# Attention and two feed-forward layers on one core: value matmuls one item later, rotation work moved, fewer weight tiles converted during attention

## The chip, the cores and the metric

One core of one Trainium2 chip runs the whole program in one launch. The metric is device time in microseconds (us). Engines are named as in the profile: PE (TensorE, with PEld for its weight loads), DVE (VectorE), ACT (ScalarE), POOL (GpSimd), SP (SyncE, which here issues all DMAs).

## What is computed

Attention over 4 batches x 8 heads x 576 positions x 64, with rotary positions, then two feed-forward layers on 2304 tokens of 512, hidden size 2048. All in fp32.

```python
def _attn_ref(q, k, v):                       # rotate(x): halves x1, x2 -> x1*cos - x2*sin, x1*sin + x2*cos
    q_rot, k_rot = (rotate(q), rotate(k))
    scores = scale * np.matmul(q_rot, k_rot.transpose(0, 1, 3, 2))
    scores = scores - np.max(scores, axis=-1, keepdims=True)
    attn = np.exp(scores)
    attn = attn / (np.sum(attn, axis=-1, keepdims=True) + 1e-09)
    return np.matmul(attn, v)
x = attention as (2304, 512)
h = x @ w_in;   g = where(h > 0, h, exp(min(h, 0)) - 1);   x = g @ w_out      # first layer
h = x @ w2_in;  g = h - tanh(h);                           out = g @ w2_out   # second layer
```

## The kernel before

The program has two stages, and in both the order of every instruction is written out by hand; each engine takes its own instructions in that order.

**Attention.** The 32 heads go in 16 pairs (`p`). A pair has 9 items (`items`, L207 and below): 128 query rows of one head each, for four row blocks `u` and two heads, and a last item with the 64 rows that remain of both heads. In the loop over items, iteration `i` does for different items, in this order: the maximum of item `i` on DVE (`emit_max`, L220), the score matmuls of item `i + 1` on PE (`emit_s`, L211; ten matmuls in a pair's last item, four in the others), the exponential of item `i` on ACT (`emit_exp`, L234), the copies of transposed scores out of PSUM that the iteration before left (`flush`, on DVE at L265 or ACT at L267), the sums' reciprocals on DVE and the normalizing on POOL for item `i - 1` (`emit_norm`, L247 to L251, only after a pair of heads is complete), rotation and conversion steps, the transposes of item `i - 4` on PE (`emit_t`, L291, the corners at L304 and L297), and value matmuls that are due (`emit_pv`, L325). There are two PSUM tiles for scores, three for transposes and one for the values' output. `PV_AT` says how many iterations after the transposes of a group of items its value matmuls stand: for each of five pieces of 128 keys a number.

```python
            PV_AT = ((1, 1, 1, 3, 3), (1, 1, 1, 3, 3), (2, 2, 2, 2, 2))
```

The rotation of q and k (`prep`) has five steps for each pair and each of q (`x` = 0) and k (`x` = 1): two multiplications with the tables on POOL (L146), an addition on DVE (L148), a rounded copy on ACT (L151), the rest on DVE (L156), and then DMAs that put the result into its operand tiles (`place`, L178 and L181). `sched` says in which iteration each stands, `early` does so for the first two pairs after the start.

**Weights.** The weights come as 64-bit numbers, in 64 tiles of 128 x 512. `load_w` loads a raw tile; `conv_w` makes fp32 of it and splits it into two fp32r parts, in `NCV` = 5 parts: absolute value on ACT (L83), two operations on DVE (L85, L86), one (L90), one (L94), and last a rounding on ACT (L102) with the remainder on POOL (L103). The eight tiles that the first layer needs first are converted during attention, one for every two pairs of heads, one part in every second iteration.

**Feed-forward.** A step is one block of 128 hidden units for 384 tokens: `emit_f1` (L445, 12 matmuls), the activation on ACT and DVE, the split of its result `g` on ACT and POOL (`emit_split`), and four steps later `emit_f2` (L503). Four steps share a token tile. The tokens' operands `x1` to `x5` are made from the attention's output during the first steps (`split_x`, ACT at L54 and POOL at L55): step `i` makes piece `i % 4` of token tile `i // 4 + 1`. Meanwhile the other 56 tiles are converted, a tile in three steps.

## Time and profile before

| | |
|---|---|
| median of 3 runs | 1132.71 us (1131.9 to 1133.64) |
| profiled execution | 1132.65 us, span 1130.9 us |
| PE busy | 1097.3 us (97%) |
| DVE, ACT, POOL busy | 765.6, 688.6, 671.3 us |
| chain that ended last, by engine | PE 90%, DVE 5%, DMA 2%, ACT 2% |
| attention stage | the first 318.6 us of the span |

The profile is of one execution. Times in the trace are in us from the span's start. "Busy" for PE includes matmuls whose operands are late, since matmuls are pipelined and their ends are modelled; how fast PE really goes is read from how often a given instruction comes round. A wait is named by what ended it.

### The profile page before, as it was taken

Reading aid. Unit: us, or ns where it says so; the run is one execution under the profiler, and the core shown is the slowest. Engines: PE = TensorE matmul, PEld = TensorE weight load, DVE = VectorE, ACT = ScalarE, POOL = GpSimd, SP = SyncE. Lnnn points to the kernel's source line nnn. Section 1 sums busy time; section 2 is a strip of 40 time slices with the busy share of each in tenths; the row PEclk is TensorE's granted clock in tenths of the full one; section 3 lists DMA queues with packets and bytes.
Section 4 is the critical chain, followed back from the end, with each engine's and each line's share of the span. In section 5 each row is a group of like instructions: output and inputs, shape, how many; then the busy total and the mean of one; then the engine's idle time right before and its main releaser. Section 6 shows DMA issues by size and latency. Waiting matters only on the chain.

```text
span 1130.9 us, 18518 instructions
## 1 busy us (share of the span) xinstructions
PE 1097.3 (97%) x6656; PEld 987.2 (87%) x6656; DVE 765.6 (68%) x1393; ACT 688.6 (61%) x1477; POOL 671.3 (59%) x609
## 2 busy tenths in 40 slices
PE   2899999999999999999999999999999999999998
PEld 2777776777799999999999999998998899899987
DVE  6988888888645434555545556678768877877665
ACT  3676766676745533333333344688888788877774
POOL 2877887887556533333333466676666666666443
PEclk9999999999999999999999999999999999999999
DMA  7767676865211111112111121111111111110102
GB/s 232 217 193 200 181 215 169 222 172 164 72 39 38 40 55 38 38 38 55 40 38 38 38 57 38 39 38 38 57 38 38 38 56 38 38 39 1 57 35 78
DMA packets 29627, 91.96 MB, mean 81 GB/s; under 512 B 4192, under 2 KB 4192, under 8 KB 29536
## 3 DMA queue, kind: packets, MB, share of 16 engines
q1 hardware_dynamic: 29536, 90.78, 28.3%
q8 instruction: 53, 0.87, 0.3%
q14 instruction: 38, 0.31, 0.1%
HBM read 57.74 MB, written 4.72 MB: 55 GB/s over the span
## 4 chain that ended last, share of the span: by engine, by line
PE 90%; DVE 5%; DMA 2%; ACT 2%; SPq 1%; issue 1%; ACTq 0%; DVEq 0%
PE h L445 36%; PE y L503 18%; PE y L505 17%; PE o L325 8%; PE s L211 6%; PE pt L291 4%; DVE nm L220 2%; DMA k<-hl 1%; ACT a L234 1%; DVE t L148 1%; DVE aT L265 1%; ACT aT L267 1%; DVE hl L156 0%; DMA tabs<-in_tab 0%; PE pr L304 0%
## 5 line engine op out<-in xcount | busy, mean ns | idle before, releaser
L445 PE MATMUL h<-x,w 128*128 128x384 f32 x2304 | 434.0, 336 | 0.0
L445 PEld LDWEIGHTS h<-x,w 128*128 128x128 f32 x2304 | 407.1, 188 | 8.0 <-ACT a L234 0.4
L488 POOL TENSOR_TENSOR g<-f,g 128x384 fp32r<-128x384 f32 x192 | 213.6, 1113 | 187.8 <-ACT g L487 182.5
L503 PE MATMUL y<-g,w 128*128 128x384 f32 x1152 | 219.0, 339 | 0.0
L505 PE MATMUL y<-w,g 128*128 128x512 f32 x864 | 216.7, 395 | 0.2 <-ACT xa L520 0.2
L503 PEld LDWEIGHTS y<-g,w 128*128 128x128 f32 x1152 | 204.0, 188 | 0.0
L505 PEld LDWEIGHTS y<-w,g 128*128 128x128 f32 x864 | 161.5, 188 | 31.9 <-ACT xa L520 0.6
L251 POOL TENSOR_SCALAR a<-a,r 128x576 f32<-128x576 f32 x144 | 135.2, 951 | 63.7 <-DVE r L248 43.6
L464 POOL TENSOR_TENSOR w<-w,u 128x384 f32<-128x384 f32 x96 | 105.4, 1098 | 99.7 <-ACT w L463 99.7
L234 ACT ACTIVATE a<-s,nm 128x576 f32<-128x576 f32 x144 | 107.1, 743 | 89.6 <-DVE nm L220 75.1
L487 ACT CAST g<-f 128x384 fp32r<-128x384 f32 x192 | 98.0, 510 | 94.1 <-PE y L503 92.4
L475 DVE TENSOR_SCALAR f<-f 128x384 f32<-128x384 f32 x96 | 40.0, 416 | 145.4 <-ACT f L456 145.4
L456 ACT ACTIVATE f<-h 128x384 f32<-128x384 f32 x96 | 47.2, 492 | 146.7 <-PE h L445 143.8
L220 DVE TENSOR_REDUCE nm<-s 128x1 f32<-128x576 f32 x144 | 108.2, 753 | 38.1 <-PE s L211 36.5
L103 POOL TENSOR_TENSOR w<-f,w 128x512 fp32r<-128x512 f32 x64 | 82.6, 1291 | 54.4 <-ACT w L102 54.3
L522 DVE TENSOR_TENSOR xa<-y,xa 128x384 f32<-128x384 f32 (+1 forms) x126 | 74.0, 612 | 47.3 <-PE y L503 42.0
L479 DVE TENSOR_TENSOR f<-h,f 128x384 f32<-128x384 f32 x96 | 53.1, 553 | 68.3 <-ACT f L465 67.8
L481 DVE COPY_PREDICATED f<-mask,w 128x384 f32<-128x384 uint32 x96 | 92.2, 961 | 10.3 <-DVE w L480 0.5
L325 PE MATMUL o<-aT,v 128*64 128x256 f32 (+1 forms) x768 | 89.3, 339 | 2.6 <-ACT aT L267 2.4
L146 POOL TENSOR_TENSOR t<-t,tabs 128x576 f32<-128x576 f32 x59 | 86.3, 1463 | 8.2 <-DMA t<-in_qk 8.2
L291 PE MATMUL pt<-ident,a 128*128 128x128 f32 x576 | 88.3, 277 | 0.1
L461 ACT ACTIVATE u<-h 128x384 f32<-128x384 f32 x96 | 47.4, 494 | 66.4 <-PE h L445 52.1
(55 smaller groups left out, 1379.2 us busy)
## 6 DMA issues: line engine op xcount, KB each, us to landing
k<-hl SPq DMA_DIRECT2D x64, 288.0 KB, 4.2
t<-in_qk SPq DMA_DIRECT2D x30, 576.0 KB, 6.2
raw<-in_w1i SPq DMA_DIRECT2D x16, 512.0 KB, 3.7
raw<-in_w1o SPq DMA_DIRECT2D x16, 512.0 KB, 3.7
raw<-in_w2i SPq DMA_DIRECT2D x16, 512.0 KB, 3.6
raw<-in_w2o SPq DMA_DIRECT2D x16, 512.0 KB, 3.6
v<-in_v SPq DMA_DIRECT2D x16, 288.0 KB, 4.7
qa<-hl SPq DMA_DIRECT2D x32, 144.0 KB, 4.0
```

The lines of the kernel that those rows point to most:

```text
L220: nc.vector.tensor_reduce(out=nm, in_=s_t[i][:, :, 0:288], axis=AX.XY, op=ALU.max, negate=True)
L234: nc.scalar.activation(out=a.rearrange("p (x c) -> p x c", x=2), in_=s[:, :, 0:288], func=AF.Exp, bias=nm_t.pop(i), scale=1.0, accum_out=den,)
L251: nc.gpsimd.tensor_scalar(out=a, in0=a, scalar1=r[:, x:x + 1], scalar2=1.0, op0=ALU.mult, op1=ALU.mult)
L291: nc.tensor.transpose(pt[:, c, :], a[:, h or 0, c0:c0 + 128], ident)
L325: nc.tensor.matmul(out=o[sl, 0:n], lhsT=w, rhs=m, start=(c == 0), stop=(c == 4))
L445: nc.tensor.matmul(out=hp, lhsT=w[:, wp, ws], rhs=x_t[t][:, xp, c, :], start=(m == 0), stop=(m == 3 * KC - 1))
L464: nc.gpsimd.tensor_tensor(out=w, in0=w, in1=u, op=ALU.mult)
L481: nc.vector.copy_predicated(f, mask.bitcast(U32), w)
L487: nc.scalar.copy(out=g[:, 0, :], in_=f)
L488: nc.gpsimd.tensor_tensor(out=g[:, 1, :], in0=f, in1=g[:, 0, :].bitcast(F32), op=ALU.subtract)
L503: nc.tensor.matmul(out=y_t[e][:, 0:NB], lhsT=w[:, wp, es], rhs=gt[:, gp, :], start=st, stop=sp)
L505: nc.tensor.matmul(out=y_t[e], lhsT=gt[:, gp, es], rhs=w[:, wp, :], start=st, stop=sp)
```

## The change

The diff, cut to its core:

```diff
-    NCV = 5
+    NCV = 6
     def conv_w(key, slot, part):
...
         elif part == 1:
             nc.vector.tensor_scalar(out=f, in0=f, scalar1=LO_CLAMP, scalar2=HI_CLAMP, op0=ALU.max, op1=ALU.min)
+        elif part == 2:
             nc.vector.tensor_scalar(
                 out=fu, in0=fu, scalar1=3, scalar2=0x3FFFFFFF, op0=ALU.logical_shift_left, op1=ALU.bitwise_and
             )
...
+    conv = [(0, kind, c) for kind in range(2) for c in range(NJ)]
+    conv += [(l, kind, NJ * g + j) for l in range(2) for g in range(NG) for j in range(NJ) for kind in range(2)][2 * NJ:]
+    NFIRST = NJ + 1
...
-        first_w = [(0, kind, c) for c in range(NJ) for kind in range(2)]
+
+        CYC, CV_AT = 28, (5, 8, 12, 17, 21, 24)
...
-                when = [i0 + o for o in ((-10, -6, -4, -3, -2, -1), (-7, -2, 0, 2, 3, 4))[x]]
+                when = [i0 + o for o in ((-10, -7, -6, -4, -3, -2), (-7, -2, -1, 1, 2, 3))[x]]
...
-            PV_AT = ((1, 1, 1, 3, 3), (1, 1, 1, 3, 3), (2, 2, 2, 2, 2))
+            PV_AT = ((2, 2, 2, 4, 4), (2, 2, 2, 4, 4), (3, 3, 3, 3, 3))
...
-                if i == 1 or i % (2 * NI) == 12:
-                    load_w(first_w[nw.pop()]) if nw else None
+                key, at = divmod(i, CYC)
+                key = conv[key] if key < NFIRST else None
+                if key and at == 0:
+                    load_w(key)
...
-                    c = NI * (p % 2) + r - 3
-                    if c >= 0 and c % 2 == 0 and c // 2 < NCV and p // 2 < len(first_w):
-                        key = first_w[p // 2]
-                        conv_w(key, key[2], c // 2)
+                    if key and at in CV_AT:
+                        conv_w(key, key[2], CV_AT.index(at))
...
-    conv = [(l, kind, NJ * g + j) for l in range(2) for g in range(NG) for j in range(NJ) for kind in range(2)]
-    conv = conv[2 * NJ:]
+    conv = conv[NFIRST:]
...
-            while nload < len(conv) and nload <= i // 3:
-                load_w(conv[nload])
-                nload += 1
-            while ndone < len(todo) and ndone < (i - 2) * NCV // 3:
+            upto = NCV * min(i + 1, 2 * NJ - NFIRST) + max(0, (i - 2) * NCV // 3)
+            while ndone < min(len(todo), upto):
+                while nload < len(conv) and nload <= ndone // NCV + 1:
+                    load_w(conv[nload])
+                    nload += 1
```

A conversion has six parts now, each with one DVE instruction at most. Five tiles are converted during attention, one in 28 items; the remaining three are converted whole in steps 0, 1 and 2 of the first layer, and the other 56 at the old rate. All value matmuls stand one item later. The rotation's DVE steps stand in iterations 5 and 7 (q) and 1 and 3 (k) of a pair; reciprocals stand in iterations 0, 2, 4, 6 and 8. The line numbers of the changed kernel are some six higher.

In attention, on PE: one pair's rows from its seventh transposes on. `s` are scores, `pt` and `pr` transposes, `o` the values' output; `qa0` and `qb0` are the two heads' queries. Before:

```order
L325 MATMUL o_709<-aT2_699,v_286 64x64 x8
L325 MATMUL o_709<-aTr2_700,v_286 64x64 x2
L211 MATMUL s_783<-k1_482,qb0_98 128x288 x4
L291 MATMUL pt_801<-ident_93,a_665 128x128 x4
L211 MATMUL s_810<-k0_479,qa0_96 128x288 x4
L211 MATMUL s_810<-k1_482,qb0_98 128x288 x2
L211 MATMUL s_810<-k1_482,qb0_98 128x224 x2
```

And in the changed kernel:

```order
L217 MATMUL s_761<-k1_469,qb0_98 128x288 x4
L297 MATMUL pt_782<-ident_93,a_656 128x128 x4
L331 MATMUL o_735<-aT_595,v_284 64x256 x2
L331 MATMUL o_735<-aTr_596,v_284 64x256 x2
L331 MATMUL o_735<-aT2_700,v_284 64x64 x8
L331 MATMUL o_735<-aTr2_701,v_284 64x64 x2
L217 MATMUL s_805<-k0_466,qa0_96 128x288 x4
L217 MATMUL s_805<-k1_469,qb0_98 128x288 x2
L217 MATMUL s_805<-k1_469,qb0_98 128x224 x2
```

The value matmuls stood two score tiles ahead of the pair's long score tile (the one with ten matmuls), and now stand right ahead of it; the next block of value matmuls likewise moves behind one more score tile.

In the first pair, on DVE: `nm` are maxima, `f` the tile that is converted. Before:

```order
L220 TENSOR_REDUCE nm_244<-s_222 128x1
L265 COPY aT_237<-pt_239 128x4x128
L85 TENSOR_SCALAR f_216<-f_216 128x512
L86 TENSOR_SCALAR f_216<-f_216 128x512
L220 TENSOR_REDUCE nm_263<-s_246 128x1
```

And in the changed kernel:

```order
L226 TENSOR_REDUCE nm_242<-s_220 128x1
L271 COPY aT_235<-pt_237 128x4x128
L226 TENSOR_REDUCE nm_261<-s_244 128x1
L271 COPY aTr_236<-pr_259 128x128
L253 TENSOR_SCALAR den_226<-den_226 128x1 x2
```

The two conversion instructions are gone from between the two maxima.

At the start of the first layer, on ACT: `x1` are pieces of the second token tile, L456 (then L462) the exponentials of the steps, L83 and L103 the first and the last ACT part of a conversion. Before:

```order
L54 CAST x1_4304<-xa_67 128x384
L456 ACTIVATE f_4332<-h_4317 128x384
L54 CAST x1_4304<-xa_67 128x384
L456 ACTIVATE f_4351<-h_4336 128x384
L54 CAST x1_4304<-xa_67 128x384
L487 CAST g_4370<-f_4332 128x384
L456 ACTIVATE f_4373<-h_4355 128x384
L54 CAST x1_4304<-xa_67 128x384
```

And in the changed kernel:

```order
L54 CAST x1_4271<-xa_67 128x384
L462 ACTIVATE f_4299<-h_4284 128x384
L83 ACTIVATE f_4305<-raw_4301 128x512
L103 CAST w1_1_4311<-f_4305 128x512
L54 CAST x1_4271<-xa_67 128x384
L462 ACTIVATE f_4329<-h_4314 128x384
L83 ACTIVATE f_4335<-raw_4303 128x512
L103 CAST w1_2_4341<-f_4335 128x512
L54 CAST x1_4271<-xa_67 128x384
L493 CAST g_4359<-f_4299 128x384
L462 ACTIVATE f_4362<-h_4344 128x384
L83 ACTIVATE f_4368<-raw_4333 128x512
```

The next row there is the third `L103 CAST`, and only then comes the fourth `x1`. Between an L83 and its L103 stand, on DVE, the four other parts of that tile.

## Rows read from the trace of the kernel before

**Rows 1.** Busy time by stretches (us): PE, PEld, DVE, ACT, POOL, clock, DMA.

```profile
100.00:150.00 50.00, 48.91 (x403) 36.55 (x402) 44.16 (x98) 33.76 (x86) 40.35 (x37) 1.00 0.73 192
...
400.00:450.00 50.00, 50.00 (x286) 50.00 (x285) 21.52 (x44) 19.23 (x40) 17.04 (x17) 1.00 0.14 40
```

**Rows 2.** PE in order of time: start, us, what; one row a pair.

```profile
45.70 0.33 PE L297 MATMUL pr<-ident,a 64*64 64x64 f32 x4
...
192.11 0.33 PE L297 MATMUL pr<-ident,a 64*64 64x64 f32 x4
209.24 0.33 PE L297 MATMUL pr<-ident,a 64*64 64x64 f32 x4
...
298.73 0.33 PE L297 MATMUL pr<-ident,a 64*64 64x64 f32 x4
```

**Rows 3.** Waits, 40 to 300 us: us in total, times, longest.

```profile
PEld o L325 <- ACT aT L267: 8.2, 14, 1.9
...
PEld pr L297 <- ACT aT L267: 3.7, 3, 1.4
...
PEld s L211 <- ACT a L234: 2.7, 8, 0.4
```

**Rows 4.** Instructions in order of time around one long score tile.

```profile
162.19 0.78 PE L211 MATMUL s<-k,qa 128*128 128x288 f32 x4
...
164.61 0.74 ACT L234 ACTIVATE a<-s,nm 128x576 f32<-128x576 f32 x1
...
165.09 1.06 PEld L325 LDWEIGHTS o<-aT,v 128*64 128x64 f32 x12 [0.17 <-issue]
```

**Rows 5.** Instructions in order of time, in the first pair.

```profile
29.18 2.96 POOL L146 TENSOR_TENSOR t<-t,tabs 128x576 f32<-128x576 f32 x2
...
29.56 1.32 DVE L85 TENSOR_SCALAR f<-f 128x512 f32<-128x512 f32 x1
...
30.91 1.50 DVE L86 TENSOR_SCALAR f<-f 128x512 uint32<-128x512 uint32 x1
...
32.34 0.74 DVE L220 TENSOR_REDUCE nm<-s 128x1 f32<-128x576 f32 x1
...
33.20 0.74 ACT L234 ACTIVATE a<-s,nm 128x576 f32<-128x576 f32 x1 [3.47 <-DVE nm L220]
...
34.08 0.80 PE L211 MATMUL s<-k,qa 128*128 128x288 f32 x4 [3.04 <-ACT a L234]
```

**Rows 6.** Busy time of a stretch behind that; granted clock is third from last.

```profile
35.00:40.00 5.00, 5.00 (x31) 3.80 (x29) 4.51 (x12) 3.92 (x10) 3.91 (x3) 0.66 0.91 327
```

**Rows 7.** Instructions in order of time, start of the first layer.

```profile
322.58 0.49 ACT L456 ACTIVATE f<-h 128x384 f32<-128x384 f32 x1 [1.18 <-PE h L445]
...
324.67 0.49 ACT L456 ACTIVATE f<-h 128x384 f32<-128x384 f32 x1 [0.78 <-PE h L445]
...
325.64 1.01 POOL L55 TENSOR_TENSOR x<-xa,x 128x384 fp32r<-128x384 f32 x1
...
328.35 0.42 DVE L85 TENSOR_SCALAR f<-f 128x512 f32<-128x512 f32 x1
328.46 2.12 PEld L503 LDWEIGHTS y<-g,w 128*128 128x128 f32 x12
```

**Rows 8.** Instructions in order of time: parts of conversions in the first layer.

```profile
472.98 0.61 ACT L102 CAST w<-f 128x512 fp32r<-128x512 f32 x1
...
473.67 1.29 POOL L103 TENSOR_TENSOR w<-f,w 128x512 fp32r<-128x512 f32 x1 [1.58 <-ACT w L102]
...
477.21 0.67 ACT L83 ACTIVATE f<-raw 128x512 f32<-128x512 f32 x1
...
480.90 0.43 DVE L86 TENSOR_SCALAR f<-f 128x512 uint32<-128x512 uint32 x1
481.36 0.69 DVE L90 SCALAR_TENSOR_TENSOR f<-raw,f 128x512 uint32<-128x512 uint32 x1
...
482.83 0.68 DVE L94 SCALAR_TENSOR_TENSOR f<-raw,f 128x512 uint32<-128x512 uint32 x1
```

More of the change, by code (lines that the diff above doesn't have):

```diff
@@ L70, in attention_elu_tanhshrink @@
     cv_t = {}
-    NCV = 5
+    NCV = 6
     def conv_w(key, slot, part):
         l, kind, c = key
-        if part < 4:
+        if part < 5:
             words = raw_t[key].bitcast(U32).rearrange("p (n t) -> p n t", t=2)
@@ L88, in conv_w @@
             )
-        elif part == 2:
+        elif part == 3:
             nc.vector.scalar_tensor_tensor(
@@ L92, in conv_w @@
             )
-        elif part == 3:
+        elif part == 4:
             nc.vector.scalar_tensor_tensor(
@@ L371, in attention_elu_tanhshrink @@
             pend = []
-            nw = list(range(len(first_w)))[::-1]
             emit_s(0)
-            PV_AT = ((1, 1, 1, 3, 3), (1, 1, 1, 3, 3), (2, 2, 2, 2, 2))
+            PV_AT = ((2, 2, 2, 4, 4), (2, 2, 2, 4, 4), (3, 3, 3, 3, 3))
             for i in range(3, 5):
```

## The prediction

> **What bounds the kernel now.** I read the busy time by stretches first. In both stages TensorE is the engine that is always busy [rows 1]: in the feed-forward stage 50 of 50 us, with 286 matmuls in 50 us, which is 0.175 us each; nothing is left to gain there, and whatever stops TensorE there is paid in full. In the attention stage it shows 48.9 of 50 us, but a matmul that waits counts as busy, so I then measured the pace from one pair of heads to the next, by the instruction that each pair has once, the corner transpose of its last item [rows 2]. From 45.70 to 298.73 there are 14 pairs, 253.0 us or 18.07 us a pair; the pair between 192.11 and 209.24, with the same instructions, took 17.13. So some 0.94 us of a pair is waiting, 14 x 0.94 = 13.2 us in all. The waits name it [rows 3]: the value matmuls (L325) and the corner transpose (L297) stand behind ScalarE's copies of transposed scores out of PSUM (L267), 8.2 and 3.7 us on the weight loads, while the score matmuls wait for an exponential only 2.7 us. Two places stand apart: a gap near 31 us [rows 5], and the seam between the stages [rows 7].
>
> **The change, part by part.**
>
> *Value matmuls one item later.* Now the copies that they need are issued, in each item, before that item's transposes and value matmuls, but the last of them comes from the transposes of the item just before. One item later those copies are an item old. The wait on L267 should go, and the corner transpose, which now has value matmuls ahead of it in the item before, should wait less too. That is worth at most the 13.2 us above. What is late next: each pair has one item whose scores take ten matmuls (both heads' last 64 rows). Its exponential must end before TensorE may write the next but one score tile, as there are two. Today a block of value matmuls stands between, and hides it; the change moves that block behind those score matmuls. In the pair at 162 us [rows 4] the long scores begin at 162.19, the next item's scores and transposes follow, and value matmuls load from 165.09 after 0.17 of issue: without them scores could have begun at 164.92. The exponential ends at 164.61 + 0.74 = 165.35, and 0.14 passes from an exponential to the score matmul that it frees (34.08 - 33.20 - 0.74, [rows 5]). So scores begin at 165.49, 0.57 late. A rotation copy on ScalarE at that spot is moved away, which may give 0.16 back; between 0.41 and 0.57 I take 0.55, since the maxima on VectorE can only add: 14 x 0.55 = 7.7 us. **Attention pace: -13.2 + 7.7 = -5.5 us**, with bounds of -13.2 (nothing late next) and 0 (VectorE's work for the rotation, with maxima behind it, takes the place of the whole).
>
> *Rotation work in items without reciprocals.* The same instructions, other items; DMAs of a pair are issued in another order on SyncE (query rows before the next pair's loads), with the key copies one item earlier. TensorE waits for no such copy after 45 us, so I cost it at nothing; its cover is the item or two by which keys land early. Its worth is in the line above: it puts the rotation under long value blocks.
>
> *Five tiles in single parts.* In the first pair, VectorE today converts a weight tile ahead of a maximum: 1.32 and 1.50 us, while GpSimd multiplies for the rotation from 29.18 on [rows 5]. The maximum behind them starts at 32.34, where it could have started at 29.56: 2.8 us, and TensorE stands still for 3.04. After it the granted clock falls: 0.66 on average over 35 to 40 us [rows 6], so some of it at 1.2 GHz, which is 0.34 x 5 = 1.7 us of work lost. The change has no VectorE part of a conversion there. Most that can come back is 2.8 + 1.7 = 4.5. But GpSimd multiplies until 29.18 + 2.96 = 32.14, and the next normalizing, which transposes wait for, stands behind that: it leaves 34.08 - 32.14 = 1.9. **Between 1.9 and 4.5 I take -3.0 us**, near the middle. The other parts lie beside other work; I cost them at nothing, within the bounds of the first line.
>
> *Three tiles at the start of the first layer.* This is where I expect to pay. In steps 0, 1 and 2 the whole conversion of a tile stands on ScalarE between an exponential and the next copy of x, and ScalarE takes its instructions in order: absolute value 0.67, then VectorE's four parts 0.42 + 0.43 + 0.69 + 0.68, then the rounding 0.61, for which ScalarE waits [rows 7, 8]. That is 3.50 us a tile, 10.5 for three. Step 4 is the first on the second token tile and needs all four copies of x; the fourth stands behind the third conversion. Today ScalarE idles 1.18 and 0.78 us in that stretch, waiting for matmuls [rows 7]; that 1.96 is absorbed. GpSimd makes the third tile's low part (1.29) before the fourth x. Handovers, six a tile at about 0.04 (481.36 - 480.90 - 0.43 = 0.03 between two parts, a little more from engine to engine), are 0.7, and I add 0.5 for one part that meets GpSimd. Slack: the fourth x is ready at 325.64 + 1.01 = 326.65 today, and the two matmuls that need it end when step 0's second matmuls load, at 328.46; so they begin at 328.1, 1.45 later. Sum: 10.5 - 1.96 + 1.29 + 1.2 - 1.45 = **9.6 us** in which TensorE stands. Bounds: 8 (handovers hidden) and 11.5 (the second part slow in all three tiles: 1.50 for 0.43). Behind that, all is as before: TensorE is full to the end, so none comes back. The second raw tile is loaded when attention's memory is free, as today's is; it lands before its turn.
>
> The stop is longer than the one at 31 us, so I expect the clock to fall in the same way: **1.7 us**, bounds 0 and 3.4 (twice that).
>
> The row of the second part shows 0.43 us alone and 1.50 with GpSimd at work [rows 5, 8]. The Trainium skill, in "SBUF — State Buffer", section "Who interferes with whom", says that VectorE and GpSimd share a port pair under an exclusive lock, and that whoever comes second blocks for the other's whole instruction. The rows agree. By that rule the second and third tile can each meet a 1.0 us GpSimd copy, 2.0 us for my 0.5, and the time would be 1136.9.
>
> **Sum.** -5.5 - 3.0 + 9.6 + 1.7 = +2.8. The profiled execution took 1132.65 us, span 1130.9 and 1.75 around it; the median of the runs is 1132.71, the same. Forecast **1135.4 us**, slightly slower. From no change, 0.2% (2.3 us) can be told.
>
> **Rivals.**
> *Attention runs at its free pace.* If the long scores cost nothing (maxima come early enough, because VectorE has three conversions less), the pace falls to 17.13: -13.2 - 3.0 + 11.3 = -4.9, 1127.8. For it: such pairs exist today, with 17.13. Against: rows 4. It decides when the mean pair is under 17.5 us. This ends faster. Chance 0.22.
> *The score loop takes the place of the wait.* VectorE's maxima, queued behind rotation work, hold the scores in every pair and the pace stays at 18: 0 - 3.0 + 11.3 = +8.3, 1141.0. For it: rows 5 show what one maximum held back costs, and it takes no more than a late operand from GpSimd in each pair. Against: the pair of 17.13 carried the same rotation work. Chance 0.18.
> *The seam costs less than half,* 4 us without a fall of the clock, because the conversions start before TensorE gets there: -8.5 + 4 = -4.5, 1128.2. Against: the absolute value stands behind step 0's exponential. Chance 0.08.
>
> **How the numbers follow.** Forecast 0.52, with its own range 1132 to 1139, about half of it over 1135 (slower), nearly half within 0.2%, a little under. The first and third rival are mostly faster, the second slower. Slower 0.27 + 0.18 + 0.01 = 0.46; faster 0.03 + 0.16 + 0.05 = 0.24; same 0.30. The range, 1126.5 to 1141.5, takes in all four points and ends just beyond the first and the second rival; the bounds of the clock's and the seam's terms lie within it.
>
> **What would show it.** Right: no wait of L325 on L267; a wait of the score matmuls for the exponential once a pair, after the long item, and pairs of 17.6 to 17.8 us; no gap at 31 us; TensorE still for 8 to 11 us before the first layer's step 4, with ScalarE's rounding waiting for VectorE's last part three times and a stretch at 1.2 GHz behind it. Wrong: pairs at 17.1 or over 18, or step 4 starting within 4 us of its place.

## The result, and the profile of the changed kernel

The changed kernel takes 1146.95 us, the median of 4 runs (1145.91 to 1147.75), against 1132.81 for the kernel before in the same comparison: ratio 1.0124, 95% interval 1.0107 to 1.0142. It is slower, and outside the forecast's range (1126.5 to 1141.5). Its profiled execution took 1147.75 us with a span of 1145.97, so 15.1 us of span have to be found. Cut at a few instructions that both kernels have (the corner transposes of [rows 2], the end of the last value matmul, the first value that a feed-forward step accumulates, `y`), they lie here:

| stretch of the span | before, us | after, us | difference | forecast |
|---|---|---|---|---|
| to the corner transpose of [rows 2] | 45.70 | 44.73 | -0.97 | -3.0 |
| 14 pairs from there | 253.03 | 257.93 | +4.90 | -5.5 |
| to the end of the last value matmul | 19.98 | 19.11 | -0.87 | 0 |
| from there to the first `y` matmul | 9.92 | 20.07 | +10.15 | +9.6 |
| the next 60 `y` matmuls | 21.13 | 22.65 | +1.52 | +1.7 |
| the rest | 781.11 | 781.48 | +0.37 | 0 |

The seam came as forecast; attention, which should have paid for it, got slower. The pace, PE in order of time (start, us, what), as in [rows 2]:

```profile
44.73 0.33 PE L303 MATMUL pr<-ident,a 64*64 64x64 f32 x4 [1.28 <-DVE aT L271]
...
63.27 0.33 PE L303 MATMUL pr<-ident,a 64*64 64x64 f32 x4
...
85.44 0.33 PE L303 MATMUL pr<-ident,a 64*64 64x64 f32 x4 [0.76 <-ACT aT L273]
...
302.66 0.33 PE L303 MATMUL pr<-ident,a 64*64 64x64 f32 x4
```

That is 18.42 us a pair in place of 18.07. One pair took 22.17 (63.27 to 85.44), the other thirteen 18.14. The waits of 40 to 300 us of the changed kernel (us in total, times, longest), to be read beside [rows 3]:

```profile
DVE nm L226 <- PE s L217: 19.8, 19, 2.6
PEld s L217 <- ACT a L240: 19.5, 38, 2.3
DVE t L154 <- POOL t L152: 13.2, 19, 1.4
DVE hl L162 <- ACT hl L157: 9.6, 15, 0.9
```

The wait of the value matmuls on ScalarE's copies is gone, all 8.2 us of it; the corner transpose's wait on them is nearly as it was (2.8 us for 3.7). In their place the score matmuls wait for the exponential, 19.5 for 2.7. Two rows are new among the long ones, VectorE's addition of the rotation waiting for GpSimd's multiplication and its last rotation step waiting for ScalarE's rounding. Before, the same two waits were short (same view and stretch, kernel before):

```profile
DVE nm L220 <- PE s L211: 29.3, 50, 1.6
...
DVE hl L156 <- ACT hl L151: 2.9, 6, 0.7
...
DVE t L148 <- POOL t L146: 1.9, 6, 0.4
```

So VectorE used to wait mostly for scores before a maximum (29.3 us, now 19.8); now more of its waiting is in rotation steps, with a maximum behind them. The two steps have also become longer, as the groups by line of 40 to 300 us show (count, busy us, mean ns of one, idle before); first the kernel before, then the changed one:

```profile
L156 DVE SCALAR_TENSOR_TENSOR hl<-t,hl 128x576 fp32r<-128x576 f32 x27 | 27.3, 1010 | 4.3 <-ACT hl L151 2.9 <-DMA t<-in_qk 0.6
L148 DVE TENSOR_TENSOR t<-t 128x576 f32<-128x576 f32 x27 | 23.1, 857 | 2.0 <-POOL t L146 1.9
```

```profile
L162 DVE SCALAR_TENSOR_TENSOR hl<-t,hl 128x576 fp32r<-128x576 f32 x27 | 32.1, 1190 | 9.9 <-ACT hl L157 9.6
L154 DVE TENSOR_TENSOR t<-t 128x576 f32<-128x576 f32 x27 | 31.1, 1151 | 13.3 <-POOL t L152 13.2
```

How one such step holds the scores is seen in order of time at 170 us of the changed kernel:

```profile
168.54 1.46 POOL L257 TENSOR_SCALAR a<-a,r 128x576 f32<-128x576 f32 x2 [1.64 <-ACT aTr L273]
...
169.97 1.42 POOL L152 TENSOR_TENSOR t<-t,tabs 128x576 f32<-128x576 f32 x1
...
171.41 1.29 DVE L154 TENSOR_TENSOR t<-t 128x576 f32<-128x576 f32 x1 [0.86 <-POOL t L152]
...
172.63 0.68 DVE L91 SCALAR_TENSOR_TENSOR f<-raw,f 128x512 uint32<-128x512 uint32 x1
...
173.24 0.74 DVE L226 TENSOR_REDUCE nm<-s 128x1 f32<-128x576 f32 x1
174.07 0.74 ACT L240 ACTIVATE a<-s,nm 128x576 f32<-128x576 f32 x1 [2.76 <-DVE nm L226]
...
174.96 0.79 PE L217 MATMUL s<-k,qa 128*128 128x288 f32 x4 [0.40 <-ACT a L240]
```

GpSimd's second multiplication of the keys stands behind a normalizing that itself waited 1.64 us. VectorE stands 0.86 us for that multiplication, which ends at 171.39, adds for 1.29, does a part of a conversion for 0.68, and only then comes the maximum for which ScalarE has waited 2.76 us. The score matmul waits 0.40 us for that exponential.

The pair of 22.17 us has the costliest such place, at 62 us:

```profile
62.59 3.29 POOL L152 TENSOR_TENSOR t<-t,tabs 128x576 f32<-128x576 f32 x2
62.69 1.92 DVE L162 SCALAR_TENSOR_TENSOR hl<-t,hl 128x576 fp32r<-128x576 f32 x1 [0.84 <-ACT hl L157]
...
64.54 1.90 DVE L95 SCALAR_TENSOR_TENSOR f<-raw,f 128x512 uint32<-128x512 uint32 x1
...
66.36 0.74 DVE L226 TENSOR_REDUCE nm<-s 128x1 f32<-128x576 f32 x1
...
67.20 0.74 ACT L240 ACTIVATE a<-s,nm 128x576 f32<-128x576 f32 x1 [3.07 <-DVE nm L226]
...
68.08 0.80 PE L217 MATMUL s<-k,qa 128*128 128x288 f32 x4 [1.87 <-ACT a L240]
```

A rotation step (1.92) and a part of a conversion (1.90, in the first layer 0.69) run beside two multiplications of 3.29 us together, and the maximum comes after both. The rotation step had waited 0.84 us, for ScalarE's rounding this time. TensorE stands 1.87 us there, and then the granted clock falls (busy time of a stretch; granted clock third from last):

```profile
68.00:72.00 4.00, 3.92 (x19) 3.56 (x21) 3.12 (x9) 3.68 (x10) 2.92 (x4) 0.59 0.73 179
```

At the start of the first layer the chain that the prediction drew is there (instructions in order of time, as in [rows 7]):

```profile
327.03 0.62 ACT L103 CAST w<-f 128x512 fp32r<-128x512 f32 x1 [2.41 <-DVE f L95]
...
332.22 0.62 ACT L103 CAST w<-f 128x512 fp32r<-128x512 f32 x1 [2.49 <-DVE f L95]
...
333.30 0.44 PE L451 MATMUL h<-x,w 128*128 128x384 f32 x1 [2.48 <-ACT x L54]
...
335.10 1.19 POOL L494 TENSOR_TENSOR g<-f,g 128x384 fp32r<-128x384 f32 x1
335.46 1.11 DVE L87 TENSOR_SCALAR f<-f 128x512 uint32<-128x512 uint32 x1
...
338.06 0.62 ACT L103 CAST w<-f 128x512 fp32r<-128x512 f32 x1 [3.17 <-DVE f L95]
...
339.14 0.69 PE L451 MATMUL h<-x,w 128*128 128x384 f32 x1 [2.94 <-ACT x L54]
```

ScalarE's rounding waits 2.41, 2.49 and 3.17 us for VectorE's last part, and step 4's matmuls wait 2.48 and 2.94 for the copies of x behind it. The granted clock is 0.50 then, which is 1.2 GHz (the last matmul above already takes 0.69 us for 0.44), and TensorE is full afterwards:

```profile
340.00:345.00 5.00, 3.97 (x12) 3.97 (x13) 4.18 (x6) 2.37 (x5) 5.00 (x6) 0.50 0.16 61
...
400.00:450.00 50.00, 50.00 (x286) 50.00 (x285) 20.78 (x40) 21.11 (x45) 19.27 (x18) 1.00 0.14 42
```

### The profile page after: what moved, and what is told of

Its sections match the earlier page's. It is cut to its first block, busy times and chain, and to the rows that moved or that the text cites. A ratio compares the mean times of both kernels' runs of the same rounds, so it can differ in the third digit from the quotient of the medians.

```text
span 1146.0 us, 18500 instructions
## 1 busy us (share of the span) xinstructions
PE 1101.0 (96%) x6656; PEld 988.6 (86%) x6656; DVE 756.6 (66%) x1393; ACT 687.3 (60%) x1477; POOL 654.5 (57%) x609
## 4 chain that ended last, share of the span: by engine, by line
PE 80%; DVE 8%; DMA 4%; POOL 3%; ACT 3%; issue 1%; SPq 1%; ACTq 0%; POOLq 0%; DVEq 0%
PE h L451 34%; PE y L509 18%; PE y L511 17%; PE o L331 5%; PE s L217 5%; DVE nm L226 2%; PE pt L297 2%; DVE hl L162 2%; DMA t<-in_qk 2%; POOL a L257 1%; ACT a L240 1%; DMA k<-hl 1%; POOL t L152 1%; DVE t L154 1%; ACT hl L157 1%
## 5 line engine op out<-in xcount | busy, mean ns | idle before, releaser
L451 PEld LDWEIGHTS h<-x,w 128*128 128x128 f32 x2304 | 407.6, 188 | 17.4 <-ACT x L54 6.2
L494 POOL TENSOR_TENSOR g<-f,g 128x384 fp32r<-128x384 f32 x192 | 207.1, 1079 | 197.5 <-ACT g L493 194.3
L257 POOL TENSOR_SCALAR a<-a,r 128x576 f32<-128x576 f32 x144 | 120.9, 852 | 76.8 <-DVE r L254 46.8
L470 POOL TENSOR_TENSOR w<-w,u 128x384 f32<-128x384 f32 x96 | 101.8, 1061 | 102.9 <-ACT w L469 102.9
L85 DVE TENSOR_SCALAR f<-f 128x512 f32<-128x512 f32 x64 | 28.3, 442 | 173.1 <-ACT f L83 173.1
L462 ACT ACTIVATE f<-h 128x384 f32<-128x384 f32 x96 | 47.2, 492 | 143.7 <-PE h L451 141.4
L152 POOL TENSOR_TENSOR t<-t,tabs 128x576 f32<-128x576 f32 x59 | 92.8, 1584 | 10.3 <-DMA t<-in_qk 6.9
L331 PE MATMUL o<-aT,v 128*64 128x256 f32 (+1 forms) x768 | 80.3, 338 | 0.0
L485 DVE TENSOR_TENSOR f<-h,f 128x384 f32<-128x384 f32 x96 | 53.0, 552 | 38.1 <-ACT f L471 37.6
```

The lines of the kernel that those rows point to most:

```text
L152: eng.tensor_tensor(out=t[:, i, :], in0=t[:, i, :], in1=tabs[:, i, :], op=ALU.mult)
L257: nc.gpsimd.tensor_scalar(out=a, in0=a, scalar1=r[:, x:x + 1], scalar2=1.0, op0=ALU.mult, op1=ALU.mult)
L331: nc.tensor.matmul(out=o[sl, 0:n], lhsT=w, rhs=m, start=(c == 0), stop=(c == 4))
L451: nc.tensor.matmul(out=hp, lhsT=w[:, wp, ws], rhs=x_t[t][:, xp, c, :], start=(m == 0), stop=(m == 3 * KC - 1))
L470: nc.gpsimd.tensor_tensor(out=w, in0=w, in1=u, op=ALU.mult)
L494: nc.gpsimd.tensor_tensor(out=g[:, 1, :], in0=f, in1=g[:, 0, :].bitcast(F32), op=ALU.subtract)
```

## The experiments

All times are medians; ratios are to the kernel before. "Attention ends" is the end of the last value matmul in the span: 318.71 before, 321.77 in the changed kernel. Seam is the time from there to the first `y` matmul: 9.92 and 20.07. Repeats of one attention order in different runs (three below) ended within 0.95 us of each other, so a difference under 1 us in the end of attention shows nothing.

### The three parts one by one and two by two

Value matmuls alone, on the kernel before:

```diff
-            PV_AT = ((1, 1, 1, 3, 3), (1, 1, 1, 3, 3), (2, 2, 2, 2, 2))
+            PV_AT = ((2, 2, 2, 4, 4), (2, 2, 2, 4, 4), (3, 3, 3, 3, 3))
```

> The value matmuls one item later, nothing else of the change. Theory A (the rotation's new places are what slows attention in the changed kernel): the waits of L325 on L267 go, the long score tile's wait comes, so 4 to 9 us less than before, 1124 to 1129. Theory B (the moved block uncovers the score loop, and that is what slows attention): as before or slower, 1132 to 1138, with pairs of 18.1 us or more.

1133.09 us, ratio 1.0006 (0.9997 to 1.0015); attention ends at 319.56, with 18.18 us a pair: theory B's range. The wait on the copies went, and the waits of scores took its whole place: on the weight loads 9.1 us for exponentials and 8.9 for copies, where it had been 2.7 and 0.4. With the rotation in its old items the move gains nothing.

Rotation alone, on the kernel before:

```diff
-    for o in ((-10, -6, -4, -3, -2, -1), (-7, -2, 0, 2, 3, 4))[x]]
+    for o in ((-10, -7, -6, -4, -3, -2), (-7, -2, -1, 1, 2, 3))[x]]
```

> The rotation's new items, nothing else of the change. Theory A: slower than before by 4 to 9 us, 1137 to 1142, with VectorE's addition (L148) waiting for GpSimd's multiplication (L146) in most pairs, over 8 us in all, against 1.9 before. Theory B: within 2 us of before, 1131 to 1135, and that wait under 4 us.

1155.59 us, ratio 1.0207 (1.019 to 1.0224); attention ends at 342.06, 23.4 us later and beyond both theories. The part that had been costed at nothing costs by far the most when it stands alone. In its waits, 40 to 300 us:

```profile
PEld o L325 <- ACT aT L267: 18.5, 13, 2.9
...
DVE t L148 <- POOL t L146: 3.8, 8, 0.7
```

The addition's wait for GpSimd is 3.8 us, far under theory A's 8: it is not what costs here. With the value matmuls still in their old place, it is they that stand (18.5 us for 8.2): ScalarE's copies are queued behind an exponential, and that behind a maximum held by a rotation step and, in this place, by a part of a conversion (instructions in order of time):

```profile
195.62 1.41 DVE L156 SCALAR_TENSOR_TENSOR hl<-t,hl 128x576 fp32r<-128x576 f32 x1 [0.72 <-ACT hl L151]
...
196.95 0.68 DVE L90 SCALAR_TENSOR_TENSOR f<-raw,f 128x512 uint32<-128x512 uint32 x1
...
197.55 0.75 DVE L220 TENSOR_REDUCE nm<-s 128x1 f32<-128x576 f32 x1
...
198.34 0.74 ACT L234 ACTIVATE a<-s,nm 128x576 f32<-128x576 f32 x1 [2.03 <-DVE nm L220]
...
199.69 1.05 PEld L325 LDWEIGHTS o<-aT,v 128*64 128x64 f32 x10 [1.98 <-ACT aT L267]
```

Conversions alone (the changed kernel with old `PV_AT` and old rotation):

```diff
-            PV_AT = ((2, 2, 2, 4, 4), (2, 2, 2, 4, 4), (3, 3, 3, 3, 3))
+            PV_AT = ((1, 1, 1, 3, 3), (1, 1, 1, 3, 3), (2, 2, 2, 2, 2))
-    for o in ((-10, -7, -6, -4, -3, -2), (-7, -2, -1, 1, 2, 3))[x]]
+    for o in ((-10, -6, -4, -3, -2, -1), (-7, -2, 0, 2, 3, 4))[x]]
```

> Five tiles in single parts during attention and three at the start of the first layer, with value matmuls and rotation as before. If the seam costs what the trace of the changed kernel shows (12 us from the end of attention's last matmul on) and the first pair gives back 3: 1140 to 1144. Rival (the seam is only long there because attention ended in another order): under 1136. Attention itself should end 2 to 5 us earlier than before.

1143.08 us, ratio 1.0092 (1.0077 to 1.0107). Attention ends at 316.61, 2.1 earlier; the seam takes 20.07. So the seam is the work of the three tiles alone.

Three pairs of parts: value matmuls and conversions (old rotation),

> The changed kernel without the rotation's new items. If the rotation is what slows attention: attention ends between 316 and 318.7 us, as with the conversions alone, and the whole takes 1142 to 1145. Rival (the moved value matmuls and the new conversions are what slows it together): 1146 to 1148, attention ending after 321.

rotation and conversions (old `PV_AT`),

> The changed kernel with the value matmuls at their old place. The rotation alone cost 23 us beside the old conversions. If that came from rotation and conversion steps in the same items: attention ends before 326 us here, and the whole takes 1144 to 1152. Rival (it came from rotation steps in items that hold value matmuls, whose copies then come late): attention ends after 334, 1160 or more.

and both moves without the new conversions, each with the lines of the diffs above.

> The kernel before with value matmuls one item later and rotation work in its new items, conversions as before (eight tiles in five parts during attention, nothing at the seam). Theory: the scores' waits for exponentials, behind VectorE's work, take the whole place of the removed waits on ScalarE's copies, with or without new conversions; then attention ends at 318.5 to 322 us and the time is 1132.5 to 1136. Rival: the two moves together bring what was predicted, and it is the new conversion parts that meet the rotation steps and take it back; then attention ends at 313 to 317 and the time is 1127 to 1131.

They took 1144.79 (ratio 1.0106, 1.0091 to 1.0122), 1160.09 (1.0243, 1.0229 to 1.0257) and 1146.89 us (1.013, 1.0113 to 1.0146). The first lies in its theory's range (the rotation is what slows attention), the second in its rival's, but for an end of attention of 333.93 where over 334 was expected. The ends of attention, side by side:

| | old value matmuls | one item later |
|---|---|---|
| old rotation, old conversions | 318.71 | 319.56 |
| old rotation, new conversions | 316.61 | 318.20 |
| new rotation, old conversions | 342.06 | 335.35 |
| new rotation, new conversions | 333.93 | 321.77 |

The rotation's move costs 23.4, 15.8, 17.3 or 3.6 us, the last only with both others beside it. The run of both moves fell outside both its ranges: the old conversions, whose VectorE parts stand in items 5 and 7 of every second pair, where q's rotation steps now stand too, meet them there (five of these seven pairs take 20.2 to 21.7 us). The new conversions, which shift by an item from tile to tile, take 13.6 us of that away. So the parts can't be priced one by one.

### Which of the rotation's instructions

Only GpSimd's multiplications moved, on the kernel before:

```diff
+    for o in ((-10, -7, -6, -3, -2, -1), (-7, -2, -1, 2, 3, 4))[x]]
```

> The kernel before, with only GpSimd's multiplications for the rotation in their new items (two neighbouring items for each of q and k), VectorE's and ScalarE's rotation steps in their old ones. The rotation as a whole, with nothing else of the change, moved the end of attention from 318.7 to 342.1 us. Theory: it is VectorE's two steps in the new items that cost, since they stand ahead of the maximum of an item whose value matmuls are not yet moved; then attention ends here at 317 to 321 us and the time is 1131 to 1135. Rival: it is the neighbouring multiplications, which slow VectorE for twice as long at a stretch; then attention ends at 336 to 342 and the time is 1150 to 1156.

1133.55 us, ratio 1.0013 (1.0004 to 1.0022); attention ends at 321.21, 2.5 later. The other 20.9 of the 23.4 come only with VectorE's and ScalarE's steps. (The time is in the first theory's range, the end of attention at its edge.)

And the changed kernel with the multiplications in their old items, the other steps in the new ones:

```diff
-    for o in ((-10, -7, -6, -4, -3, -2), (-7, -2, -1, 1, 2, 3))[x]]
+    for o in ((-10, -6, -4, -4, -3, -2), (-7, -2, 0, 1, 2, 3))[x]]
```

> The changed kernel with GpSimd's four multiplications of a pair in their old items (two items apart), the rotation's other steps in the new ones. If the neighbouring multiplications are what slows attention there (VectorE's addition waits for them, its two-operand steps run beside them): that wait falls from 13 us to under 6, attention ends 2 to 4 us earlier, 1142 to 1145. Rival (the items of VectorE's own steps matter): 1146 to 1149.

1162.97 us, ratio 1.0269 (1.0254 to 1.0283); attention ends at 337.02, later than both expectations. Parting the two multiplications did not help; this edit also brings the second of them closer to VectorE's addition. Here q's addition stands in the very item of the second multiplication and k's in the next, and VectorE waits in all 27 additions (40 to 300 us):

```profile
DVE t L154 <- POOL t L152: 50.8, 27, 2.8
...
PEld s L217 <- ACT a L240: 39.2, 65, 1.9
```

37.6 us more of this wait stand beside 15.3 us more of attention. That is the first size for the theory which most of the rest tests: VectorE, in order, waits for GpSimd with the maxima behind it.

### Meetings of conversions and rotation

All eight tiles in attention, in 18 items each, the rest as in the change:

```diff
-    NFIRST = NJ + 1
+    NFIRST = 2 * NJ
-        CYC, CV_AT = 28, (5, 8, 12, 17, 21, 24)
+        CYC, CV_AT = 18, (3, 5, 7, 9, 11, 15)
```

> The changed kernel, but all eight tiles converted during attention, in single parts, one tile in 18 items; nothing is converted whole in the first steps of the first layer. If the seam costs 12 us and three more tiles cost attention up to 3: 1135 to 1138. Rival (three more tiles on a full VectorE cost attention as much as the seam did): over 1142.

1137.92 us, ratio 1.0049 (1.0034 to 1.0064); seam 9.92 as before, attention ends at 323.00. Without the seam 9.0 us are back, and what is left of the loss is in attention.

One part of the first tile, the L95 of 64.54 us above, one item later:

```diff
+                    cv_at = CV_AT if i >= CYC else (5, 8, 12, 17, 22, 24)
```

> The whole change, with one part of the first weight tile's conversion (its second scalar_tensor_tensor on VectorE) one item later, and nothing else moved. In the changed kernel one pair of heads took 22.17 us (63.27 to 85.44) where the others took 18.14 on the average, and that part, 1.90 us long, stood in it behind a rotation step of 1.92 and ahead of a maximum. Theory: this one meeting on VectorE, and the half clock behind it, are the 4 us; then that pair takes 17.9 to 18.6 here, attention ends at 317.3 to 318.3, and the time is 1142.5 to 1144. Rival: the rotation step and the two neighbouring multiplications are enough for it, or the stretch at half clock has another cause; then the pair stays over 21 us, attention ends at 321 to 322.5, and the time is 1146 to 1148.

1145.69 us, ratio 1.0118 (1.0104 to 1.0131). The pair fell from 22.17 to 19.51, no stretch at 1.2 GHz was left in attention, and it ends at 319.38, 2.4 us earlier. That lies between the two expectations: this one meeting is most of what attention had lost (2.4 of 3.1 us), but not all that the pair had over the others.

Conversion parts out of all items with rotation steps:

```diff
-        CYC, CV_AT = 28, (5, 8, 12, 17, 21, 24)
+        CYC, CV_AT = 27, (5, 8, 11, 15, 22, 24)
```

> The whole change, with a conversion every 27 items in place of 28, and its parts placed so that VectorE's four never stand in an item that has a rotation step of VectorE. The score loop by itself: attention ends at 318.5 to 320 us (19.4 was reached by moving one part of one tile), time 1144.5 to 1146. Meetings of conversions and rotation on VectorE: attention ends at 314 to 317.5, time 1139.5 to 1143.5. The start of the first layer is that of the whole change, 11 to 12 us, in either case.

1144.21 us, ratio 1.0107 (1.0093 to 1.0121); attention ends at 318.65, with 18.13 us a pair. Without meetings attention ends where it did in the kernel before, and nothing is won: the first theory's end of attention.

Two runs with the old value matmuls and rotation and eight tiles in single parts, first `CYC, CV_AT = 18, (5, 8, 10, 12, 14, 16)`, then `18, (3, 5, 10, 12, 16, 17)` (both with `NFIRST = 2 * NJ`):

> The kernel before with conversions in single parts (six), but all eight tiles during attention, one in 18 items, and nothing at the start of the first layer; value matmuls and rotation as before. Theory: single parts bring 1 to 2 us in attention (five tiles alone brought 2.1), and without the three tiles the seam costs nothing: attention ends at 316.8 to 318.2 and the time is 1130.5 to 1132, faster than before by 0.05 to 0.2%. Rival: what five tiles brought came from VectorE and GpSimd having three conversions less; then eight tiles give 318.5 to 320 and 1132.5 to 1134.

> The order of before for value matmuls and rotation, eight tiles in six single parts during attention, one in 18 items, with VectorE's four parts only in items that have neither a rotation step nor a reciprocal; nothing at the start of the first layer. Eight tiles in single parts cost 5.3 us when two of the parts stood in such items. Theory: those meetings were the cost; then attention ends at 316.5 to 318.7 and the time is 1130.5 to 1132.7. Rival: six single parts of eight tiles are themselves too much ahead of the maxima; then 321 to 324 and 1135 to 1138.

1138.48 (ratio 1.0054, 1.0041 to 1.0067) and 1138.71 us (1.0056, 1.0042 to 1.0069); attention ends at 324.03 and 323.27. The first run missed both its theories; the second is near its rival (eight tiles are themselves too much ahead of the maxima: 321 to 324 and 1135 to 1138). Five tiles in single parts gain between 1.1 and 2.1 us in attention (three runs), eight lose 5, wherever these two tables put them. Why is not settled.

### VectorE's wait for GpSimd

As the run with parts kept apart, and the multiplications one item earlier:

```diff
-    for o in ((-10, -7, -6, -4, -3, -2), (-7, -2, -1, 1, 2, 3))[x]]
+    for o in ((-10, -8, -7, -4, -3, -2), (-7, -3, -2, 1, 2, 3))[x]]
```

> The whole change with conversion parts kept out of the items with rotation steps (attention ended at 318.65 us, as late as before the change), and GpSimd's multiplications for the rotation one item earlier, so that two items lie between the second of them and VectorE's addition in place of one. Theory: VectorE, in order, waits there for GpSimd (11.6 us in 17 waits between 40 and 300 us) with the maxima behind it, and this is what holds the scores; then that wait falls under 4 us, the wait of the score matmuls for the exponential (16.5 + 3.2 us) by a third or more, attention ends at 314 to 317 and the time is 1139.5 to 1143. Rival: two score tiles hold the pace whatever VectorE does, or the normalizing on GpSimd now comes late in its place; then attention ends at 318 to 321 and the time is 1143.5 to 1147.

1144.05 us, ratio 1.0102 (1.0084 to 1.012); attention ends at 316.99 and eight of fourteen pairs take 17.6 to 17.7. The time is in the rival's range, the end of attention at the edge of the theory's (the stretch behind the seam was 0.9 us dearer here than in the run with parts kept apart). The waits (40 to 300 us):

```profile
POOL t L152 <- DMA t<-in_qk: 21.8, 10, 3.9
...
DVE t L154 <- POOL t L152: 6.9, 6, 2.1
```

The addition's wait is down from 11.6 to 6.9, not under the 4 of the theory, and the score matmuls' for the exponential from 19.7 to 13.1 (weight loads and matmuls), by the third expected; but GpSimd has come to stand before its loads. The last run moves these loads two items earlier and spreads the seam's conversions:

```diff
+    for o in ((-12, -8, -7, -4, -3, -2), (-9, -3, -2, 1, 2, 3))[x]]
-            upto = NCV * min(i + 1, 2 * NJ - NFIRST) + max(0, (i - 2) * NCV // 3)
+            upto = (1, 5, 6, 11, 13, 17)[i] if i < 6 else 18 + min(5 * (i - 6) // 2, 2 * (i - 2))
```

> The changed kernel with the four places mended that the runs have named: conversion parts out of the items with rotation steps, one tile in 27 items; GpSimd's multiplications one item earlier; the loads of q and k two items earlier, since the multiplications then waited 21.8 us in 10 waits for them; and the three tiles at the start of the first layer spread over steps 0 to 6. Theory: attention runs at 17.6 us a pair in nearly all pairs and ends at 314 to 316.5 us, the seam costs 0.5 to 1.5 us, and the time is 1128 to 1131.5, faster than both kernels. Rival: the waits only move again, to reciprocals or the exponential; then attention ends at 317 to 319 and the time is 1132 to 1135.

1129.36 us, ratio 0.9981 (0.9972 to 0.999): faster than both kernels. Attention ends at 312.99, earlier than expected. Waits of 40 to 300 us, and the corner transposes in order of time:

```profile
PEld s L217 <- ACT a L240: 12.0, 29, 1.0
...
POOL t L152 <- DMA t<-in_qk: 1.3, 1, 1.3
...
DVE t L154 <- POOL t L152: 0.8, 1, 0.8
```

```profile
45.28 0.33 PE L303 MATMUL pr<-ident,a 64*64 64x64 f32 x4 [1.62 <-DVE aT L271]
...
221.28 0.33 PE L303 MATMUL pr<-ident,a 64*64 64x64 f32 x4
...
293.88 0.33 PE L303 MATMUL pr<-ident,a 64*64 64x64 f32 x4
```

From 45.28 to 221.28 ten pairs take 17.60 us each, and all fourteen 17.76 on the average. Of the 4.0 us that attention ends ahead of the run before, 3.0 are in these pairs. The score matmuls' wait for the exponential is no shorter than there (13.8 us for 13.1); the addition's is.

Eight kernels have the change's value matmuls and VectorE steps. In seven of them the addition's wait and the end of attention go together: 50.8 and 337.02, 16.5 and 323.00 (eight tiles in attention), 13.2 and 321.77, 13.2 and 319.38 (one part moved), 11.6 and 318.65, 6.9 and 316.99, 0.8 and 312.99. The eighth, with the old conversions, has 17.4 and 335.35: meetings of conversions with rotation cost by themselves, as the two kernels with 13.2 show as well. The other signs that the steps are held do not go with the end: in the last kernel the rotation's last step still waits 7.7 us for ScalarE's rounding, and the two steps still take 1133 and 1025 ns (9.6 us, 1190 and 1151 ns in the changed kernel).

### The seam spread

On the run with conversions alone, three parts a step from step 0:

```diff
-            upto = NCV * min(i + 1, 2 * NJ - NFIRST) + max(0, (i - 2) * NCV // 3)
+            upto = min(3 * (i + 1), NCV * (2 * NJ - NFIRST)) + max(0, (i - 2) * NCV // 3)
```

> Value matmuls and rotation as before, five tiles during attention in single parts, and the three tiles at the start of the first layer at three parts a step instead of six, so that the rounding of a tile stands a step after its absolute value. If ScalarE's waiting for a whole conversion makes the seam's stop: the stop falls from 10 us to 0 to 3 and the clock stays up, 1129 to 1133. Rival (VectorE and GpSimd are simply overloaded there): the stop stays over 6, 1137 or more.

1139.28 us, ratio 1.006 (1.0047 to 1.0073): the time is the rival's. The seam fell to 12.86, but two stretches at 1.2 GHz of 3.4 us each followed, and the 60 `y` matmuls behind took 26.25 us in place of 21.13. With ScalarE's rounding never in the step of VectorE's last part:

```diff
+            upto = (1, 5, 7, 11, 13, 17)[i] if i < 6 else 18 + min(5 * (i - 6) // 2, 2 * (i - 2))
```

> Five tiles during attention in single parts, value matmuls and rotation as before; the three tiles at the start of the first layer are spread over steps 0 to 6 so that ScalarE's rounding never stands in the step of VectorE's last part: one part in step 0, four, two, four, two, four, one. Theory: the seam's cost is ScalarE's wait, in order, for VectorE's four parts; with a step between them TensorE stops for 0 to 1 us, no stretch at 1.2 GHz follows, and the time is 1130.3 to 1132 (attention ends near 316.8). Rival: whatever is converted in steps 0 to 3 delays the tokens' copies or the activations, since the engines' time itself is short there; then TensorE stops or runs slowly for 4 us or more and the time is 1135 to 1139, like the earlier spreading at three parts a step.

1133.21 us, ratio 1.0011 (1.0002 to 1.002), between the two ranges. Seam 11.84, no stretch at 1.2 GHz, the 60 matmuls 21.11. Most of the 1.9 us that stay is here, instructions in order of time:

```profile
325.32 1.41 POOL L104 TENSOR_TENSOR w<-f,w 128x512 fp32r<-128x512 f32 x1
...
326.75 0.67 ACT L83 ACTIVATE f<-raw 128x512 f32<-128x512 f32 x1 [1.62 <-POOL w L104]
...
327.32 0.50 ACT L54 CAST x<-xa 128x384 fp32r<-128x384 f32 x1
...
327.88 0.44 PE L451 MATMUL h<-x,w 128*128 128x384 f32 x1 [0.75 <-ACT x L54]
```

The second tile's absolute value waits for GpSimd's remainder of the first, and the fourth x stands behind it. With that absolute value one step later, and parts in attention at `CYC, CV_AT = 27, (5, 7, 10, 14, 21, 24)`:

> The order of before for value matmuls and rotation, five tiles in single parts kept out of items with rotation steps and reciprocals, one in 27 items, and the three tiles spread over steps 0 to 6 of the first layer: one part, four, one, five, two, four, one. The earlier spreading stopped TensorE for 1.9 us since ScalarE's absolute value of the second tile, ahead of the fourth x, waited 1.62 for GpSimd's remainder of the first; here it stands behind the fourth x. Theory: TensorE stops for under 0.5 us at the seam, attention ends at 315.5 to 317.5, and the time is 1129.5 to 1131.5. Rival: the seam still costs 1.5 or more from the engines' time in those steps: 1132 to 1134.

1132.31 us, ratio 1.0004 (0.9995 to 1.0012): the rival's range. Attention ends at 316.49, the seam takes 10.75, the 60 matmuls 21.80. The seam's extra cost is down from 11.7 us to 1.5; what it still costs eats most of the 2.2 us that attention gains, and the time can't be told from the kernel before.

## Why the prediction was wrong

**The step that failed** is the rotation's: "TensorE waits for no such copy after 45 us, so I cost it at nothing". That asked who waits for the rotation's result. It did not ask who is queued behind its steps on VectorE, and for what these steps themselves wait. The move puts k's last VectorE step into the item of q's second multiplication, beside both (62.69 above; before, it stood in the item between them), and its addition behind a multiplication that GpSimd's own queue makes late (169.97 above): the waits in VectorE's rotation steps rose from 4.8 to 22.8 us, the steps grew by 12.8 (27 of each, 294 and 180 ns longer), and each has maxima behind it. Of these the addition's wait for GpSimd and the meetings with conversion parts are what the runs tie to attention's end: with both nearly gone, in the last kernel, attention ends 8.8 us earlier than in the changed one, though the other wait and most of the extra length are still there. Next to the other two parts the move cost 3.6 us (318.20 to 321.77). Alone it cost 23.4, 20.9 of it only with VectorE's and ScalarE's steps; there the addition's wait was 3.8 us, so that cost has another make-up (copies for the value matmuls behind late maxima), shown in its waits and in one place above, and not tested by itself.

**Attention's pace, -5.5 forecast, +4.9 measured.** The pace was one term for the value matmuls and the rotation's new items together. Of the waits that it was to remove, the value matmuls' 8.2 us went and the corner transpose's stayed. With the rotation in its old items nothing was won by that: the end of attention moved by +0.9 us beside the old conversions and +1.6 beside the new (319.56 and 318.20), as waits of the score matmuls took the place. With the rotation in the new items the lateness of VectorE did: 18.13 us a pair without meetings, 18.14 in thirteen pairs of the changed kernel, and one pair at 22.17. The sum of the term was nearly right for another order: it leaves a pace of 17.68, and in the last kernel, where the addition waits 0.8 us in all and conversion parts stand apart, twelve of fourteen pairs take 17.6. There the score matmul behind each pair's long item waits for the exponential as drawn, 0.39 us on its weight load; gaps put down to issue are as long, so it is not shown that this wait makes the 17.6. The sentence "the maxima on VectorE can only add" closed the term at a bound of 0; meetings with conversions went beyond it, since VectorE's part and the fall of the clock were thought of for the old order alone. That the conversions' other parts cost nothing was the same oversight: moving one part by one item gave 2.4 us.

**The second rival had the mechanism**, but for the meetings with conversions: "VectorE's maxima, queued behind rotation work, hold the scores in every pair and the pace stays at 18", down to "a late operand from GpSimd in each pair". It had 0.18. What spoke against it, the pair of 17.13 with "the same rotation work", was no evidence: in that pair the work stood in its old items. Its time, 1141.0, was short of the measured one mostly by the pair of 22.17 us and by what the first pair did not give.

**The first pair, -3.0 forecast, -0.97 measured.** The gap at 31 us is gone, and a wait of 1.41 us for an exponential stands at 36.08 instead. The time to the first corner differs by 0.8 us between three runs of one order (44.59 to 45.38; 44.23 to 46.37 among all kernels), so no more than a gain near 1 us can be claimed: mis-sized by 2. That the conversion's two instructions set it is not shown either: the run with the value matmuls alone has them, waits 0.92 us for 3.04 with the clock at 1.00, and still comes to its first corner at 45.96.

**The seam, 9.6 + 1.7 forecast, 10.15 + 1.52 measured.** Right in place, chain and size; the second number is 1.3 to 2.4 in all eight kernels with this seam. The three waits of ScalarE's rounding, step 4 as the place and a stretch at 1.2 GHz are in the rows. Spreading the same parts, with each rounding a step behind VectorE's last part, takes 10 of 11.7 us away, which bears the in-order chain out; the spread also puts fewer parts into those steps (17 up to step 5 for 24), and no run parts the two. The upper bound was added up wrong: a second part of 1.50 in all three tiles gives 9.6 - 0.5 + 3.2 = 12.3, not 11.5, and nothing hangs on it. The 0.5 us for a part that meets GpSimd was also near: the second part took 1.11 for 0.43 once, beside a GpSimd instruction of 1.19 (335.10 above). The Trainium skill's rule on the shared port pair ("SBUF — State Buffer", section "Who interferes with whom") agrees in kind: the part began 0.36 us behind GpSimd's and ended 0.28 behind its end. The 2.0 us that the prediction worked out by it for the seam did not come, since the other two tiles' second parts met nothing.

Of the measured sum, 15.1, the seam is 11.7, attention with its first and last pair 3.1, and the rest 0.4; forecast were 11.3, -8.5 and 0.

## What to carry to other kernels

When a step is moved on an engine that takes its work in order, ask for what the moved instruction waits in its new place, and what is queued behind it there; a wait that cost nothing ahead of idle time can cost much ahead of the instruction that feeds the bottleneck (37.6 us more of it went with 15.3 us here). Price parts that share a queue together: here the same move cost 23 us or 4 by what stood beside it, and was part of a gain once its operands came earlier and conversions kept out of its way. A chain that hops between two engines inside one step belongs spread over steps, so that the engine that also feeds the bottleneck waits less in it.

## What was not expected of the hardware

VectorE's last rotation step, 0.76 us in other places, took 1.92 us and a conversion part 1.90 in place of 0.69, beside two GpSimd multiplications that themselves took 3.29 in place of 2 x 1.42: both engines lose. And the granted clock fell in the middle of attention, behind a stop of TensorE of 1.87 us: 0.59 over 68 to 72 us of the changed kernel, and in the run of both moves without the new conversions 0.52 to 0.60 over stretches near 87, 155 and 196 us, behind stops of 1.05, 2.12 and 1.95. So in these places a late maximum was paid twice. The stop of 1.41 us at 36.08 of the changed kernel was followed by no such stretch: the length of the stop alone does not tell.
